# The first MoE's g from a ring of eight shared with the decoding's temporaries, its down products three feature tiles behind the up products

## The chip, the cores and the metric

One core of one Trainium2 chip runs the whole program. The metric is device time in microseconds (us) from one launch, of the slowest core, and here there is one. The engines are named as in the profile: PE (TensorE's matmuls), PEld (its weight loads), DVE (VectorE), ACT (ScalarE), POOL (GpSimd), SP (SyncE, which issues most DMAs). Each engine takes its instructions in the order in which they stand in its own queue; an instruction that waits holds up all behind it on that engine.

## What is computed

Three stages, each feeding the next. In the attention, a 40x40 state per head is decayed, corrected and updated at each of 768 steps, for 4 batches of 8 heads. Then a first MoE layer with one expert, and a second with four:

```python
for t in range(S):                                  # S = 768, D = 40
    y[:, :, t] = einsum('bhd,bhde->bhe', r_t, state)
    Sa = einsum('bhde,bhe->bhd', state, a_t)
    state = state * w_t[:, :, None, :] - outer(Sa, b_t) + outer(v_t, k_t)
x = y.transpose(0, 2, 1, 3).reshape(3072, 320)
h = x @ w_in                                        # 320 x 2048
g = h - tanh(h)
x = g @ w_out                                       # 2048 x 320
for e in range(4):                                  # second MoE, 320 x 1024 x 320 each
    out += p[:, e:e+1] * (maximum(x @ w1[e], 0) @ w2[e])
```

`w_in` and `w_out` arrive as 64-bit floats, and the kernel decodes them itself.

## The kernel before

The 768 steps of the attention are worked in chunks of 64, for two batches at a time: 24 chunks in all. Of each chunk there are a preparation (scans on DVE over w, line 200, after a clamp in line 263; the matrix products M of line 235), an inverse of a triangular matrix by columns on POOL (lines 299 and 301), the chain that carries the state (Z line 340, U 349, R 360, U again, T 390, S 371, in this order and from chunk to chunk), and the output (SC and Y, lines 418 to 435).

The first MoE works in blocks of 256 tokens, 12 blocks. A block has 16 feature tiles f of 128 features. `up(f)` puts eight matmuls (line 528) into a PSUM tile h, of which there are two (`psH`, line 80); ACT takes tanh of it into t (line 577); DVE forms t = h - t (line 578), which is the last reader of h; ACT copies t into gh, rounded (line 579); DVE forms the remainder gl = t - gh (line 580). `down(f)` multiplies gh and gl with the weights, six matmuls (line 591), into two accumulators of the block. gh and gl have three buffers each.

The products of the second MoE (lines 528 and 1011) follow when the first is done; that stage alone is about 700 us long.

The weights of the first MoE come in 32 pieces, an up and a down for each f. A piece is loaded (line 492), decoded by one ACT and four DVE instructions (lines 454 to 459) through temporaries t0 (two buffers), t1 and f2 (one each), rounded into a high part on ACT (line 471), and what is left is summed on PE by three products into a PSUM tile (`rest`, line 478), from which ACT copies the low part (line 479). The load of a piece waits for a mark that is written behind the high part of the piece three before it (lines 174 and 501).

The source emits these steps in slots: one chunk's chain, the preparation and inverse of later chunks, the output of an earlier one, and a share of the decoding (slots up to 1.75) or of the first MoE (from slot 2 on, lines 904 to 914), spread over the slot. The order in each engine's queue is not this order: the program is built with a scheduler (line 1093) that simulates the engines and takes, of what is ready there, what was emitted first. So a change of buffers or of the emitted order moves instructions of all stages against each other.

`moe1_all` (line 613) emits up(i) and then down(i - 2); `temps` (line 876) allots the decoding's temporaries. Both draw on the pool `mp`.

Of the kernel before, what the change touches and what calls it, by code (L numbers as in the profile page):

```python
# [12 lines left out]
F32R = mybir.dt.float32r  # L13
I32 = mybir.dt.int32
# [27 lines left out]
def tile_wkv_then_moe_then_moe(ctx, tc, r, k, v, w, a, b, moe_w_in, moe_w_out, probs, w1, w2, wT, aT, rT, kbT, vP, vT, wi_in, wo_in, out):  # L42
# [419 lines left out]
    def split_weights(raw, done, key, tag, temps):  # L462
        n = raw.shape[1] // words
        if f64:
            parts = decode(raw.rearrange("p (n two) -> p n two", two=2), *temps(n))
        else:
            parts = [temps(n)[0].bitcast(F32)]
            nc.vector.tensor_copy(out=parts[0], in_=raw)
        t = done[key] = wp.tile([128, 2, n], F32R, tag=tag, name=tag)
        hi, lo = t[:, 0], t[:, 1]  # L470
        nc.scalar.activation(out=hi, in_=parts[0], func=AF.Copy)
        return parts, hi, lo
# [47 lines left out]
    def fc1(ps, w_hi, w_lo, fs, x_hi, x_lo, ts_):  # L520
        lhs = lambda t, kk: t[:, kk, fs]
        rhs = lambda t, kk: t[:, kk, ts_]
        ops = []
        for kk in range(2):
            ops += [(lhs(w_hi, kk), rhs(x_hi, kk)), (lhs(w_hi, kk), rhs(x_lo, kk)), (lhs(w_lo, kk), rhs(x_hi, kk))]
        ops += [(lhs(w_hi, 2), rhs(x_hi, 2)), (lhs(w_lo, 2), rhs(x_hi, 2))]
        for i, (l, rr) in enumerate(ops):
            nc.tensor.matmul(ps, l, rr, start=(i == 0), stop=(i == len(ops) - 1))  # L528
# [15 lines left out]
    def moe1(mp, hf, bl):  # L544
        NTB = G * 128
# [24 lines left out]
        def up(f):  # L570
            ps = psH.tile([128, NTB], F32, tag="h", name="h")
            wi_hi, wi_lo = (wi_t[f][:, h].rearrange("p (k n) -> p k n", k=3) for h in range(2))
            fc1(ps, wi_hi, wi_lo, slice(0, 128), M["xh"], M["xl"], slice(0, NTB))
            t = mp.tile([128, NTB], F32, tag="t", name="t", bufs=2)
            gh = mp.tile([128, NTB], F32R, tag="gh", name="gh", bufs=3)
            gl = mp.tile([128, NTB], F32R, tag="gl", name="gl", bufs=3)
            nc.scalar.activation(out=t, in_=ps, func=AF.Tanh)  # L577
            nc.vector.tensor_tensor(out=t, in0=ps, in1=t, op=ALU.subtract)  # L578
            nc.scalar.activation(out=gh, in_=t, func=AF.Copy)  # L579
            nc.vector.tensor_tensor(out=gl, in0=t, in1=gh, op=ALU.subtract)  # L580
            M["g", f] = gh, gl
# [16 lines left out]
        def fin_b(tt):  # L598
# [10 lines left out]
            nc.sync.dma_start(out=x1T_d[256:DM, t0:t0 + 128], in_=x1T[0:KR, 2])  # L609

        return load, up, down, fin_a, fin_b, split

    def moe1_all(mp, blocks, weights):
        def add(fn, what):
            steps.append((lambda: (weights(what), fn())) if what else fn)

        fns = [moe1(mp, hf, bl) for hf, bl in blocks]
        steps = [fns[0][0], fns[0][5]]
        loads = [0]
        seq = [(n, f) for n in range(len(blocks)) for f in range(NF)]  # L620

        def down(n, f):
            add(lambda: fns[n][2](f), ("down", f) if n == 0 else None)
            if f == NF - 1:
                for tt in range(G):
                    steps.append(lambda tt=tt: fns[n][3](tt))
            if f == 1 and n > 0:
                for tt in range(G):
                    steps.append(lambda tt=tt: fns[n - 1][4](tt))

        for i, (n, f) in enumerate(seq):
            add(lambda n=n, f=f: fns[n][1](f), ("up", f) if n == 0 else None)
            if f == LOAD_F and n + 1 < len(blocks):
                loads.append(len(steps))
                steps.append(fns[n + 1][0])
            if f == NF - 1 and n + 1 < len(blocks):
                steps.append(fns[n + 1][5])
            if i >= 2:
                down(*seq[i - 2])
        down(*seq[-2])  # L640
        down(*seq[-1])
        for tt in range(G):
            steps.append(lambda tt=tt: fns[-1][4](tt))
        return steps, loads
# [226 lines left out]
    mp = one.enter_context(tc.tile_pool(name="mp", bufs=2, side="right"))  # L871
# [2 lines left out]
    nc.scalar.activation(out=minus, in_=ident, func=AF.Copy, scale=-1.0)  # L874

    def temps(n):
        kinds = (("t0", I32, 2), ("t1", I32, 1), ("f2", F32R, 1))
        return [mp.tile([128, 384], d, tag=t, name=t, bufs=k_)[:, 0:n] for t, d, k_ in kinds]

    dec, need = weights_steps(plus, minus, temps)  # L880
    done = [0]
# [6 lines left out]
    def share(i):  # L888
        k0, k1 = (max(0, int(len(dec) * (j - DEC_FROM) / (DEC_TO - DEC_FROM))) for j in (i, i + 1))
        return [lambda k=k: decoded(k + 1) for k in range(k0, min(k1, len(dec)))], 0, 1  # L890

    msteps, mloads = moe1_all(mp, blocks, lambda what: decoded(need[what]))

    def late_loads():
# [203 lines left out]
```

## Time and profile before

| what | value |
|---|---|
| median of 3 runs | 1610.53 us (1608.2 to 1612.03) |
| the profiled execution | 1613.03 us, of which the span, first to last instruction, is 1611.3 us |
| granted TensorE clock, mean | 0.948 of full speed |
| PE / DVE / POOL / ACT busy | 92 / 50 / 36 / 31 % of the span |
| first up product of the first MoE | at 194.0 us |
| last up product of the first MoE | at 903.6 us |

The profile comes from one execution. Its times count from the first instruction. A wait is idle time of an engine before an instruction, put down to the one that released it. The shares of busy time are averages over stages with different limits, so the stages are read one by one: to about 200 us (attention and decoding), 200 to 907 us (attention and first MoE; at the end the first MoE alone), and from 907 us the second MoE.

### The profile page before, as it was taken

The numbers are of one execution on the slowest core, as the hardware profiler recorded it, in microseconds if no ns is written. First come the engines' busy times: TensorE is split into PE (matmuls) and PEld (weight loads), VectorE is DVE, ScalarE is ACT, GpSimd is POOL, SyncE is SP. The second block draws the span as 40 slices with busy tenths as digits, with TensorE's granted clock in tenths as the row PEclk, the third lists the DMA queues.
The fourth block names the chain that finished last, engine by engine and source line by source line (L and its number), as shares of the span: only waits on it lengthen the run. The fifth ranks groups of instructions, "written<-read, shape, count | busy, mean of one in ns | idle before, by whom it ended". The sixth has DMA issues, their size and how long they took to land.

```text
span 1611.3 us, 33016 instructions
## 1 busy us (share of the span) xinstructions
PE 1478.0 (92%) x13178; PEld 1330.4 (83%) x13178; DVE 807.2 (50%) x1604; ACT 503.1 (31%) x1239; POOL 586.7 (36%) x1543
## 2 busy tenths in 40 slices
PE   3587898898989899989998999999999999999998
PEld 2366698888878788879998989898898989898997
DVE  8588756665656566666556443332333333332332
ACT  3344433333333333333345462121221212121111
POOL 4888865648485484665703001000000101010000
PEclk9578799999998999999999999999999999999999
DMA  4556522332432323232215331000010101000011
GB/s 127 130 151 158 132 50 72 97 83 69 101 86 77 82 69 95 76 94 66 61 39 156 101 100 29 8 21 17 1 36 1 37 1 36 1 1 1 0 50 51
DMA packets 163938, 103.26 MB, mean 64 GB/s; under 512 B 101952, under 2 KB 139840, under 8 KB 163776
## 3 DMA queue, kind: packets, MB, share of 16 engines
q1 hardware_dynamic: 97412, 71.64, 16.1%
q10 hardware_dynamic: 66364, 29.44, 7.6%
q8 instruction: 105, 1.72, 0.4%
q14 instruction: 57, 0.47, 0.1%
HBM read 82.82 MB, written 18.22 MB: 63 GB/s over the span
## 4 chain that ended last, share of the span: by engine, by line
PE 57%; DMA 6%; POOL 5%; DVE 3%; issue 3%; ACT 1%; SPq 0%; ACTq 0%; DVEq 0%; POOLq 0%
PE h L528 26%; PE acc L1011 21%; PE acc L591 4%; POOL Y L301 2%; POOL tmp L299 2%; PE SC L418 1%; DMA E<-in_wT_dram 1%; DMA N<-mt_d 1%; DMA TT<-tt_d 1%; PE SC L429 1%; DMA tt_d<-Y 1%; PE SC L433 1%; PE M L235 1%; DMA KBT<-in_kbT_dram 1%; PE Z L340 1%
## 5 line engine op out<-in xcount | busy, mean ns | idle before, releaser
L299 POOL TENSOR_TENSOR tmp<-Y,N 128x60 f32<-128x60 f32 (+24 forms) x744 | 254.8, 343 | 208.3 <-DMA N<-mt_d 108.9
L998 DVE SCALAR_TENSOR_TENSOR hl<-h,hh 128x512 fp32r<-128x512 f32 x192 | 132.1, 689 | 332.9 <-ACT hh L997 332.8
L301 POOL TENSOR_TENSOR Y<-Y,tmp 128x60 f32<-128x60 f32 (+24 forms) x744 | 264.7, 356 | 58.3
L997 ACT ACTIVATE hh<-h 128x512 fp32r<-128x512 f32 x192 | 114.6, 598 | 505.2 <-PE h L528 505.1
L528 PE MATMUL h<-xh,up 128*128 128x256 f32 x1152 | 236.9, 301 | 24.3 <-DVE t L578 14.2
L1011 PE MATMUL acc<-w2h,hh 128*128 128x320 f32 x768 | 236.3, 308 | 0.6 <-DVE oacc L1016 0.6
L1011 PE MATMUL acc<-w2l,hh 128*128 128x320 f32 x768 | 236.4, 308 | 0.0
L1011 PE MATMUL acc<-w2h,hl 128*128 128x320 f32 x768 | 235.3, 308 | 0.2 <-DVE hl L998 0.2
L528 PE MATMUL h<-xh,w1h 128*128 128x512 f32 x576 | 227.8, 395 | 0.0
L528 PE MATMUL h<-xh,w1l 128*128 128x512 f32 x576 | 227.1, 394 | 0.0
L947 POOL TENSOR_TENSOR w1l<-w1r,w1h 128x1536 fp32r<-128x1536 f32 x8 | 28.0, 3498 | 528.4 <-ACT w1h L946 528.4
L528 PEld LDWEIGHTS h<-xh,up 128*128 128x128 f32 x1152 | 188.6, 201 | 31.4 <-DVE t L578 17.7
L591 PE MATMUL acc<-down,gh 128*128 128x320 f32 x768 | 171.3, 321 | 3.1 <-ACT gh L579 3.1
L1011 PEld LDWEIGHTS acc<-w2l,hh 128*128 128x128 f32 x768 | 144.0, 188 | 12.0
L1011 PEld LDWEIGHTS acc<-w2h,hh 128*128 128x128 f32 x768 | 144.1, 188 | 11.6 <-DVE oacc L1016 1.0
L528 PE MATMUL h<-xl,w1h 128*128 128x512 f32 x384 | 151.7, 395 | 0.0
L1011 PEld LDWEIGHTS acc<-w2h,hl 128*128 128x128 f32 x768 | 143.7, 187 | 0.7 <-DVE hl L998 0.5
L1018 DVE SCALAR_TENSOR_TENSOR oacc<-acc,pnorm,oacc 128x320 f32<-128x320 f32 x168 | 84.4, 544 | 116.2 <-PE acc L1011 116.2
L591 PEld LDWEIGHTS acc<-down,gh 128*128 128x128 f32 x768 | 124.3, 194 | 6.3 <-ACT gh L579 4.1
L577 ACT ACTIVATE t<-h 128x256 f32<-128x256 f32 x192 | 72.4, 384 | 180.9 <-PE h L528 110.6
L580 DVE TENSOR_TENSOR gl<-t,gh 128x256 fp32r<-128x256 f32 x192 | 93.4, 491 | 69.0 <-ACT gh L579 67.7
L591 PE MATMUL acc<-down,gl 128*128 128x320 f32 x384 | 113.5, 324 | 14.0 <-DVE gl L580 14.0
(138 smaller groups left out, 2317.6 us busy)
## 6 DMA issues: line engine op xcount, KB each, us to landing
N<-mt_d SPq DMA_DIRECT2D x48, 256.0 KB
KBT<-in_kbT_dram ACTq DMA_DIRECT2D x46, 160.0 KB
raw_up<-in_wi_dram SPq DMA_DIRECT2D x16, 384.0 KB
raw_down<-in_wo_dram SPq DMA_DIRECT2D x16, 320.0 KB
w2r<-in_moe_w_dram SPq DMA_DIRECT2D x8, 640.0 KB
w1r<-in_moe_w_dram SPq DMA_DIRECT2D x16, 256.0 KB
xT_d<-yT SPq DMA_DIRECT2D x48, 80.0 KB
wchk<-in_w_dram SPq DMA_DIRECT2D x5, 768.0 KB
```

Of the source, the lines that this page charges most:

```text
L235: nc.tensor.matmul(ps[:, 128 * j:128 * j + 128], KBT[:, p], zs[:, :, p], start=True, stop=True)
L299: nc.gpsimd.tensor_tensor(out=tmp, in0=Y[:, 0:n, j:j + 1].to_broadcast([128, n, wd]), in1=nj.to_broadcast([128, n, wd]), op=ALU.mult)
L301: nc.gpsimd.tensor_tensor(out=Y[:, 0:n, j + 1:32], in0=Y[:, 0:n, j + 1:32], in1=tmp, op=ALU.subtract)
L528: nc.tensor.matmul(ps, l, rr, start=(i == 0), stop=(i == len(ops) - 1))
L577: nc.scalar.activation(out=t, in_=ps, func=AF.Tanh)
L580: nc.vector.tensor_tensor(out=gl, in0=t, in1=gh, op=ALU.subtract)
L591: nc.tensor.matmul(M["acc"][tt], l[:, cs], rr, start=(f == 0 and i == 0), stop=(f == NF - 1 and i == 2))
L947: nc.gpsimd.tensor_tensor(out=w1l, in0=w1r, in1=w1h, op=ALU.subtract)
L997: nc.scalar.activation(out=hh_, in_=ps, func=AF.Relu)
L998: nc.vector.scalar_tensor_tensor(out=hl_, in0=ps, scalar=0.0, in1=hh_, op0=ALU.max, op1=ALU.subtract)
L1011: nc.tensor.matmul(po, l[:, cs], rr[:, f], start=(f == 0 and i == 0), stop=(f == FH - 1 and i == 2))
L1018: nc.vector.scalar_tensor_tensor(out=oacc[:, n], in0=po, scalar=pe, in1=oacc[:, n], op0=ALU.mult, op1=ALU.add)
```

## The change

```diff
@@ -572,8 +572,8 @@
             wi_hi, wi_lo = (wi_t[f][:, h].rearrange("p (k n) -> p k n", k=3) for h in range(2))
             fc1(ps, wi_hi, wi_lo, slice(0, 128), M["xh"], M["xl"], slice(0, NTB))
             t = mp.tile([128, NTB], F32, tag="t", name="t", bufs=2)
-            gh = mp.tile([128, NTB], F32R, tag="gh", name="gh", bufs=3)
-            gl = mp.tile([128, NTB], F32R, tag="gl", name="gl", bufs=3)
+            gh = mp.tile([128, 384], F32R, tag="g", name="gh", bufs=8)[:, 0:NTB]
+            gl = mp.tile([128, 384], F32R, tag="g", name="gl", bufs=8)[:, 0:NTB]
             nc.scalar.activation(out=t, in_=ps, func=AF.Tanh)
             nc.vector.tensor_tensor(out=t, in0=ps, in1=t, op=ALU.subtract)
             nc.scalar.activation(out=gh, in_=t, func=AF.Copy)
@@ -635,8 +635,9 @@
                 steps.append(fns[n + 1][0])
             if f == NF - 1 and n + 1 < len(blocks):
                 steps.append(fns[n + 1][5])
-            if i >= 2:
-                down(*seq[i - 2])
+            if i >= 3:
+                down(*seq[i - 3])
+        down(*seq[-3])
         down(*seq[-2])
         down(*seq[-1])
         for tt in range(G):
@@ -874,8 +875,8 @@
     nc.scalar.activation(out=minus, in_=ident, func=AF.Copy, scale=-1.0)
 
     def temps(n):
-        kinds = (("t0", I32, 2), ("t1", I32, 1), ("f2", F32R, 1))
-        return [mp.tile([128, 384], d, tag=t, name=t, bufs=k_)[:, 0:n] for t, d, k_ in kinds]
+        kinds = (("t0", I32), ("t1", I32), ("f2", F32R))
+        return [mp.tile([128, 384], d, tag="g", name=t, bufs=8)[:, 0:n] for t, d in kinds]
 
     dec, need = weights_steps(plus, minus, temps)
     done = [0]
```

The temporaries t0, t1, f2 and the tiles gh and gl now take turns in one ring `g` of eight tiles of 128x384. Before, there were four temporaries of 384 and six g tiles of 256 columns, which is the same amount of memory. A piece of the decoding takes three tiles of the ring, a feature tile of the first MoE two, so that four feature tiles' g can be held where three could. down(i - 3) is emitted after up(i) in place of down(i - 2). No product, no copy and no DMA is added or removed.

The scheduler makes another order of it. Two places, as the queues stand (names carry the number of their buffer).

On DVE, in the third block of the first MoE around feature tiles 8 and 9. Before, t_4869 and gl_4871 belong to tile 8 and t_4912 to tile 9; L263, L200 and L210 are the preparation of a later chunk:

```order
L364 TENSOR_TENSOR Z_4514<-R_4680,Z_4514 32x320 x2
L578 TENSOR_TENSOR t_4869<-h_4860,t_4869 128x256
L263 TENSOR_SCALAR E2_117<-E2_117 128x8x64
L200 SCALAR_TENSOR_TENSOR RW_102<-E2_117,delta_92 128x260 x2
L210 RECIPROCAL start_103<-RW_102 40x8 x2
L200 SCALAR_TENSOR_TENSOR E2_117<-E2_117,start_103 128x260 x2
L580 TENSOR_TENSOR gl_4871<-t_4869,gh_4870 128x256
L578 TENSOR_TENSOR t_4912<-h_4903,t_4912 128x256
```

After, t_4863 and gl_4865 belong to tile 8, t_4906 and gl_4908 to tile 9:

```order
L364 TENSOR_TENSOR Z_4524<-R_4674,Z_4524 32x320 x2
L263 TENSOR_SCALAR E2_117<-E2_117 128x8x64
L200 SCALAR_TENSOR_TENSOR RW_102<-E2_117,delta_92 128x260 x2
L210 RECIPROCAL start_103<-RW_102 40x8 x2
L353 TENSOR_SCALAR vu0_93<-U_4739 32x8x40
L578 TENSOR_TENSOR t_4863<-h_4854,t_4863 128x256
L200 SCALAR_TENSOR_TENSOR E2_117<-E2_117,start_103 128x260 x2
L578 TENSOR_TENSOR t_4906<-h_4897,t_4906 128x256
L228 TENSOR_TENSOR KBT0_100<-KBT0_100,RW_102 128x512 x2
L580 TENSOR_TENSOR gl_4865<-t_4863,gh_4864 128x256
L580 TENSOR_TENSOR gl_4908<-t_4906,gh_4907 128x256
```

t of tile 9 now stands ahead of gl of tile 8, and both gl behind the whole preparation; the end of U (L353) stands ahead of both t.

On PE, in the chain of the first chunk, with the decoding's rest products (up_ is the high part of an up piece, down_ that of a down piece, t_ and f_ temporaries). Before, from R to S:

```order
L360 MATMUL R<-vu_93,MB_112 32x40 x16
L478 MATMUL rest<-up_647,minus 128x384
L478 MATMUL rest<-f_641,plus 128x384
L478 MATMUL rest<-t_675,ident 128x320
L349 MATMUL U<-Z,TT_125 32x40 x16
L478 MATMUL rest<-down_683,minus 128x320
L478 MATMUL rest<-f_677,plus 128x320
L478 MATMUL rest<-t_717,ident 128x384
L390 MATMUL T<-ident,vu_93 128x64 x8
L371 MATMUL S<-vu_93,KBn_108 40x40 x8
```

After, from the last rest products ahead of U to S:

```order
L478 MATMUL rest<-t_743,ident 128x320
L478 MATMUL rest<-down_751,minus 128x320
L478 MATMUL rest<-f_745,plus 128x320
L478 MATMUL rest<-t_788,ident 128x384
L349 MATMUL U<-Z,TT_125 32x40 x16
L478 MATMUL rest<-up_796,minus 128x384
L478 MATMUL rest<-f_790,plus 128x384
L478 MATMUL rest<-t_835,ident 128x320
L478 MATMUL rest<-down_843,minus 128x320
L478 MATMUL rest<-f_837,plus 128x320
L390 MATMUL T<-ident,vu_93 128x64 x8
L371 MATMUL S<-vu_93,KBn_108 40x40 x16
```

Of the 96 rest products, 31 stood ahead of T of the first chunk, and now 42; ahead of T of the second, third and fourth chunk it is 50, 61 and 79, and now 55, 73 and 87. The first up product stands behind 94 of them in both. But it stood behind R of the fifth chunk, and now within Z of that chunk, two chain steps earlier; and 14 feature tiles' up products now stand ahead of T of the fifth chunk, where it was 3. From the sixth chunk on the two orders are near each other again. In the last block, with no attention beside it, down(f) stands behind up(f + 2) in both.

## Rows read from the trace of the kernel before

**Rows 1.** The page: the span, and busy time of each engine.
```profile
span 1611.3 us, 33016 instructions
...
PE 1478.0 (92%) x13178; PEld 1330.4 (83%) x13178; DVE 807.2 (50%) x1604; ACT 503.1 (31%) x1239; POOL 586.7 (36%) x1543
```

**Rows 2.** Busy time by stretch: stretch, its us, engines, TensorE clock, DMA share, GB/s.
```profile
0.00:200.00 200.00, 134.51 (x1448) 101.78 (x1448) 149.36 (x305) 82.20 (x228) 152.76 (x390) 0.77 0.53 139
200.00:907.00 707.00, 646.89 (x7883) 601.92 (x7883) 428.52 (x900) 264.55 (x753) 395.09 (x1141) 0.95 0.32 79
...
140.00:160.00 20.00, 12.98 (x142) 11.33 (x142) 15.80 (x34) 6.25 (x18) 16.71 (x43) 0.80 0.58 149
160.00:180.00 20.00, 17.40 (x169) 12.43 (x165) 15.09 (x32) 8.96 (x25) 16.47 (x46) 0.52 0.47 130
180.00:200.00 20.00, 16.68 (x246) 13.26 (x244) 13.89 (x31) 9.06 (x22) 16.62 (x44) 1.00 0.53 130
```

**Rows 3.** TensorE waits, 200 to 800 us: us in total, times, longest.
```profile
PE h L528 <- DVE t L578: 13.8, 10, 5.4
PE acc L591 <- DVE gl L580: 10.2, 11, 2.9
...
PE acc L591 <- ACT gh L579: 2.8, 3, 1.8
```

**Rows 4.** VectorE in order of time, 349 to 355.5 us: start, us, instruction.
```profile
349.72 0.42 DVE L578 TENSOR_TENSOR t<-h,t 128x256 f32<-128x256 f32 x1
350.68 0.43 DVE L263 TENSOR_SCALAR E<-E 128x512 f32<-128x512 f32 x1 [0.53 <-DMA E<-in_wT_dram]
...
354.12 0.40 DVE L580 TENSOR_TENSOR gl<-t,gh 128x256 fp32r<-128x256 f32 x1
354.43 0.41 DVE L578 TENSOR_TENSOR t<-h,t 128x256 f32<-128x256 f32 x1
```

**Rows 5.** TensorE in order of time, three places: idle time in brackets.
```profile
354.57 0.56 PE L591 MATMUL acc<-down,gl 128*128 128x320 f32 x2 [2.23 <-DVE gl L580]
...
510.79 1.44 PE L591 MATMUL acc<-down,gh 128*128 128x320 f32 x4 [1.83 <-ACT gh L579]
...
655.12 0.90 PE L591 MATMUL acc<-down,gl 128*128 128x320 f32 x2 [2.94 <-DVE gl L580]
```

**Rows 6.** Granted TensorE clock (third from the end) in two stretches, as rows 2.
```profile
510.50:517.30 6.80, 6.30 (x23) 5.51 (x24) 4.18 (x11) 2.38 (x8) 0.00 (x0) 0.50 0.48 131
653.90:660.60 6.70, 5.48 (x24) 5.40 (x25) 4.00 (x10) 2.83 (x8) 5.37 (x18) 0.50 0.25 59
```

**Rows 7.** ScalarE and TensorE in order of time, 560 to 566 us.
```profile
562.95 0.66 ACT L577 ACTIVATE t<-h 128x256 f32<-128x256 f32 x2 [8.98 <-DMA N<-mt_d]
...
563.85 0.58 PE L528 MATMUL h<-xh,up 128*128 128x256 f32 x1 [5.36 <-DVE t L578]
```

**Rows 8.** TensorE waits, 800 to 910 us.
```profile
PE acc L591 <- DVE gl L580: 3.8, 2, 2.7
```

**Rows 9.** VectorE and GpSimd in order of time, 858 to 879 us.
```profile
862.28 3.47 DVE L580 TENSOR_TENSOR gl<-t,gh 128x256 fp32r<-128x256 f32 x1 [1.14 <-ACT gh L579]
...
862.02 3.45 POOL L947 TENSOR_TENSOR w1l<-w1r,w1h 128x1536 fp32r<-128x1536 f32 x1 [59.46 <-ACT w1h L946]
```

**Rows 10.** TensorE waits for the decoding, 0 to 200 us.
```profile
PE rest L478 <- ACT down L471: 10.2, 4, 5.4
PE rest L478 <- DVE t L456: 8.2, 8, 2.3
...
PE rest L478 <- ACT up L471: 3.3, 3, 2.7
...
PE h L528 <- ACT down L479: 2.5, 1, 2.5
```

**Rows 11.** Lines 454 and 528: ns min/median/max, first to last start, in us.
```profile
L454 ACT ACTIVATE t<-raw_up x16: 524/552/568, 11.4 to 183.0; 128x384 f32<-128x384 f32 x16
...
L528 PE MATMUL h<-xh,up x1152: 274/283/583, 194.0 to 903.6; 128*128 128x256 f32 x192
```

## Prediction

> **What bounds the kernel now.** I read the page first for the whole, then the busy time by stretch, then TensorE's waits by stretch, and last the engines in order of time around single waits. PE is busy for 92% of the span, DVE for half of it [rows 1]. In the order of the stages: to 200 us PE stands idle for 200 - 134.5 = 65.5 us, and POOL works 16.5 to 16.7 of each 20 us, so it is POOL's inverses that set how fast chunks come there [rows 2]. From 200 to 907 us PE is idle for 707 - 646.9 = 60.1 us at a mean granted clock of 0.95 [rows 2]: this stretch is bound by PE's own work and by the short waits inside it, and a us of idle time that goes there comes off the end, since the second MoE only follows. The change touches the second MoE nowhere, so what is decided is decided before 907 us.
>
> The waits that the change speaks of are those of the down products: 10.2 us for gl and 2.8 us for gh between 200 and 800 us, 13.0 us in 14 waits [rows 3]. Beside them the up products wait 13.8 us in 10 waits for t, that is, for one of the two h tiles to be read [rows 3].
>
> **Term 1, the waits of the down products.** The three largest are of three kinds. At 354.6 us PE waits 2.23 us for gl [rows 5]: DVE did t at 349.7, then took up a preparation that waited for a DMA and ran to 354.1, then gl, and the next t only behind it [rows 4]. At 655.1 us it waits 2.94 us, at the end of a block, and at 510.8 us 1.83 us for gh, an ACT matter [rows 5]. Would one more tile of distance cover such a wait? With the old order on DVE, hardly: up(f + 3) needs the h tile that t of f + 1 frees, and that t stood behind the late gl (gl done 354.1 + 0.4 = 354.5, t done 354.8 [rows 4]), so PE would have got 0.9 us of other work and then stood before an up product in place of a down product. But the new order on DVE is another: in the first place shown of the change, t of two tiles in a row stand ahead of both gl, so the h tiles come free without gl, and the down products that wait for gl stand behind more up products. That covers the first kind. The second kind has the end of a block and a late load in it, the third a late ACT; I count these as not surely covered. So I take half of the 13.0 us: 6.5 us, with 0 and 13.0 as the ends.
>
> To this comes the clock. In the 6.8 us around the waits at 510.8 and 655.1 us the granted clock is 0.50, the lower of TensorE's two levels, 1.2 GHz in place of 2.4 [rows 6]; each such stretch gives back half its length, 3.4 us, if PE doesn't stop ahead of it. I take one of the two, 3.4 us, with 0 and 6.8 us as ends. Term 1 is 9.9 us of gain, between 0 and 19.8.
>
> From 800 to 910 us 3.8 us of waits for gl stay [rows 8]: there the order of up and down products is the same before and after. What made them is in the trace: a gl of 128x256 takes 3.47 us from 862.28 on, where others take 0.40 [rows 4, 9], while POOL runs one subtraction of 3.45 us from 862.02 on [rows 9]. The Trainium skill, page "SBUF — State Buffer", section "SBUF: two separate sides", says of this that VectorE instructions with two SBUF inputs and GpSimd instructions that read SBUF lock the same pair of ports for their whole length; by that rule a ring of g cannot shorten it, and the trace agrees. It leaves the sum as it is.
>
> **Term 2, waits of the up products.** What is not waited for at a down product can come back at an up product: both hang on the same DVE and ACT queues. The largest such wait, 5.36 us at 563.8 us, comes from ACT standing for 8.98 us before tanh [rows 7]; there two full h tiles stop PE whatever g's ring holds, but for one more down product that is left to do. The trace has no row for the new order, so the ends are a loss of the 6.5 us that term 1 took back, and a gain of half of the 13.8 us, 6.9 us, if the t that now stand earlier on DVE free h sooner. I take a loss of 2 us, nearer to nothing than to the lower end: of the ten waits for t [rows 3] the long one shown is ACT's doing, which the order on DVE doesn't touch.
>
> **Term 3, the decoding.** Its pieces go through three of eight ring tiles in place of fixed temporaries, so f2 of a piece no longer waits for PE's sum of the piece before it. The same number of instructions runs. The scheduler answers by putting the decoding earlier against the attention: 42 in place of 31 rest products ahead of the first chunk's T. Now the decoding ends and the first up product starts at 194.0 us [rows 11]; the 16 up pieces start between 11.4 and 183.0 us [rows 11], 171.6 / 30 = 5.7 us for a piece. If it ends earlier, the first MoE fills PE's idle time: from 140 to 200 us that is 7.0 + 2.6 + 3.3 = 12.9 us [rows 2], and that is the upper end. If it doesn't, PE, which takes its queue in order, stands before rest products that are not ready: it did so for 10.2 + 8.2 + 3.3 + 2.5 = 24.2 us already [rows 10], and half as much again, 12.1 us, is my lower end. POOL sets the pace of the chunks here and its order does not depend on the ring, so neither end is near; I take 0.
>
> **The sum.** 9.9 - 2.0 + 0 = 7.9 us of gain. The profiled execution took 1613.0 us (span 1611.3 and 1.7 us around it), so it would take 1605.1 us; the median of the runs is 2.5 us lower, 1610.5, and 7.9 us off it give 1602.6 us.
>
> **The rivals.** *It is h, not g, that is short.* The two h tiles bound how far PE runs ahead, g's ring does not, and each us saved at a down product is lost at the next up product. For it speaks that waits for t are as large as those for gl and gh together, 13.8 against 13.0 us [rows 3], and the place at 354 us with DVE's old order; against it speaks DVE's new order. The Trainium skill, page "Perfetto Trace Analysis", section "Optimization Strategy", says that gaps which come again and again on the engine that should be full can mean too little SBUF or PSUM for the next tile; by it the gap belongs to whichever ring is short, and the trace has both kinds. Time: no change, 1610.5 us. Chance 0.20.
>
> *Slower: the decoding stands in the chain's way.* In PE's queue the first chunk's T now stands behind 11 more rest products, that is 11 / 3 = 3.7 pieces, and 3.7 x 5.7 = 21 us at the old pace. If the pace stays, the chains of the first four chunks wait on PE for it, chunk five's T comes behind 14 feature tiles, and the lost time on PE is the 12.1 us of above, 1622.6 us. For it speaks that PE already waits 24.2 us for decoding [rows 10]; against it that the chain has room behind POOL, and that PE finds the first MoE's work ahead of T of chunk five. It decides from the start of the first up product: later than 194 us with PE's waits for rest grown, this rival holds. Chance 0.23.
>
> *Faster by much: the decoding ends earlier as well.* Term 1 as taken and term 3 at its upper end: 9.9 - 2.0 + 12.9 = 20.8 us, 1589.7 us. For it speaks that f2's wait is gone and that each engine's queue has the decoding earlier; against it that the loads still wait for the piece three before. Chance 0.13.
>
> **How the numbers follow.** The forecast has 0.44, around 1602.6 us, from 1597 to 1607 with its own bounds. Faster by over 0.2% (3.2 us, about what a measurement of this kernel tells from no change) come the forecast and the last rival, 0.57; within it the first rival, 0.20; slower the second, 0.23. The range leaves out 0.2 of the chances: from 1589, where the last rival lies, to 1619, short of the full price of the slower one.
>
> **What would show it.** Right: waits for gl and gh between 200 and 800 us at some 6 us in place of 13.0, those for t at 13 to 17, fewer stretches at clock 0.50, the first up product within 5 us of 194. The first rival: gl and gh down, t up by as much, PE idle from 200 to 907 us still near 60. The slower one: waits for rest of 30 us and more, the first up product after 200 us, the first MoE's last product after 907. The last: the first up product ahead of 185 us. The forecast is wrong as a whole if PE's idle time after 200 us moves by waits that no term names, for the new order moves all stages: waits of the chain for DVE and for loads.

## The result and the profile after

The changed kernel takes 1621.22 us (median of 5 runs, 1618.53 to 1621.56), the kernel before 1610.53; the ratio is 1.0062, 95% interval 1.0045 to 1.008. So it is slower by 0.6%, where 1602.6 us was forecast, and 2 us outside the range. The profiled execution has a span of 1619.8 us against 1611.3 [rows 1].

TensorE's waits of the changed kernel between 200 and 800 us (us in total, times, longest), to be read against [rows 3]:

```profile
PE h L528 <- DVE t L578: 28.0, 13, 5.9
PE T L390 <- DVE vu L353: 20.0, 6, 5.8
...
PE acc L591 <- DVE gl L580: 1.4, 2, 1.3
```

The wait for gl, 10.2 us in [rows 3], is 1.4 us, and none for gh is left. But the up products wait 28.0 us for t in place of 13.8. And the chain's T (line 390) waits 20.0 us for vu, of which the same view of before has this:

```profile
PE T L390 <- DVE vu L353: 8.0, 6, 4.2
```

Busy time by stretch and TensorE's clock (third from the end), as [rows 2], and the first and last up product, as [rows 11]:

```profile
0.00:200.00 200.00, 125.58 (x1290) 94.08 (x1290) 145.00 (x296) 78.18 (x223) 141.34 (x375) 0.78 0.51 132
200.00:907.00 707.00, 644.36 (x7982) 604.23 (x7982) 427.50 (x901) 263.53 (x749) 403.68 (x1157) 0.94 0.32 82
...
L528 PE MATMUL h<-xh,up x1152: 274/283/583, 196.9 to 912.4; 128*128 128x256 f32 x192
```

These waits do not add up to the loss. Others fell by 11.8 us: those of the up products for xh (4.8 and 2.3 us, now none), of SC for DVE (2.5, now none), of U for Z (6.7, now 5.4) and 0.9 us of Z without a releaser. So PE's idle time from 200 to 800 us went from 54.2 to 57.1 us only, and from 200 to 907 us from 60.1 to 62.6. To 200 us it is 200 - 125.6 = 74.4 us, where it was 65.5; but here executions of one order scatter. Runs below that keep an order up to about 200 us (of the experiments with `LAG` and `INV_CUT` for the old one, with four and three tiny loads for the new one) give 68.0 and 70.7 us for the old one, 69.7 and 73.4 for the new one. What holds in all six is U's wait for the load of TT, 18.3 to 19.9 us in the new order, 11.6 to 12.9 in the old.

The first up product comes 2.9 us later than in [rows 11] (in two other executions of the new order at 193.7 and 192.8 us, so this is scatter), the last 8.8 us later. In between the profiled execution was not behind: the eighth of the twelve blocks ends (its first copy of line 596) at 720.8 us, before at 724.0. The ninth ends at 788.3, before at 781.0. The third block, with a stand ahead of 350 us that is shown below, loses as much, 74.1 us long in place of 64.7; but the blocks up to the eighth win that back. The ninth is what stays lost, and the loss shows in one stretch of it, here before and then after:

```profile
720.00:740.00 20.00, 19.23 (x202) 18.03 (x202) 14.03 (x31) 9.47 (x28) 16.57 (x44) 1.00 0.16 39
740.00:760.00 20.00, 19.68 (x292) 18.15 (x290) 10.49 (x25) 7.49 (x21) 7.25 (x27) 1.00 0.39 100
```

```profile
720.00:740.00 20.00, 18.62 (x198) 17.63 (x197) 13.37 (x30) 9.77 (x29) 16.32 (x48) 0.91 0.20 45
740.00:760.00 20.00, 14.09 (x195) 12.89 (x192) 6.27 (x14) 3.60 (x10) 7.00 (x24) 0.85 0.27 61
```

From 740 to 760 us PE is idle for 5.9 us, before for 0.3, and its clock is 0.85, before 1.00. The engines in order of time (start, us, instruction, idle time before it in brackets; ACTq and SPq are the queues' own steps, DMA issues here):

```profile
742.28 0.84 ACTq L248 DMA_DIRECT2D mt_d<-MB  x2
743.16 0.43 ACT L352 ACTIVATE vu<-U 32x320 f32<-32x320 f32 x1 [0.51 <-PE U L349]
743.24 8.17 ACTq L248 DMA_DIRECT2D mt_d<-MB  x2
...
748.83 0.37 SPq L306 DMA_DIRECT2D tt_d<-Y  x1
751.13 0.58 SPq L310 DMA_DIRECT2D TT<-tt_d  x1
...
751.51 4.20 ACTq L152 DMA_DIRECT2D rd<-in_rT_dram  x2
755.80 0.38 ACT L577 ACTIVATE t<-h 128x256 f32<-128x256 f32 x1 [12.21 <-DMA TT<-tt_d]
...
756.70 0.58 PE L528 MATMUL h<-xh,up 128*128 128x256 f32 x1 [5.91 <-DVE t L578]
```

ACT has 12.21 us without work. It is not out of work: tanh stands in its queue behind four stores of MB and two loads of rd, and two of these six issues do not go out. The fourth store has gone out by 743.24 + 8.17 = 751.4, 2.6 us after SP's store of the inverse (748.83), the second load of rd by 755.7, 4.6 us after SP's load of TT (751.13). Nothing in the data ties them to these transfers. I call this "ACT stands". The changed kernel has five such stands of 9.3 to 12.2 us between 200 and 910 us; the kernel before has three of over 7 us, 8.98 us at most [rows 7].

The stand ahead of 350 us shows how T's waits grow from it:

```profile
342.02 0.37 SPq L306 DMA_DIRECT2D tt_d<-Y  x1
344.32 0.58 SPq L310 DMA_DIRECT2D TT<-tt_d  x1
...
344.69 4.51 ACTq L248 DMA_DIRECT2D mt_d<-MB  x2
349.30 0.72 ACTq L152 DMA_DIRECT2D E<-in_wT_dram  x2
...
348.22 0.76 PE L349 MATMUL U<-Z,TT 32*32 32x40 f32 x32
...
351.97 0.43 DVE L263 TENSOR_SCALAR E<-E 128x512 f32<-128x512 f32 x1 [5.70 <-DMA E<-in_wT_dram]
...
354.20 0.50 DVE L353 TENSOR_SCALAR vu<-U 32x320 f32<-32x320 f32 x1
...
354.75 0.69 PE L390 MATMUL T<-ident,vu 64*128 64x64 f32 x8 [5.77 <-DVE vu L353]
```

PE had U ready by 349. The load of E stood on ACT behind a store of MB until 349.3, so DVE waited 5.70 us for E in the preparation of a later chunk. The copy of U (line 353) stood behind that on DVE, and T behind the copy on PE.

What stayed: from 800 to 910 us the down products wait 3.6 us for gl, as in [rows 8].

```profile
PE acc L591 <- DVE gl L580: 3.6, 3, 2.4
```

### The profile page after: what moved, and what is told of

Same layout as the page of the kernel before. It is cut to its first block, busy times and chain, and to the rows that moved or that the text cites. A ratio compares the mean times of both kernels' runs of the same rounds, so it can differ in the third digit from the quotient of the medians.

```text
span 1619.8 us, 32999 instructions
## 1 busy us (share of the span) xinstructions
PE 1474.5 (91%) x13178; PEld 1333.2 (82%) x13178; DVE 805.4 (50%) x1604; ACT 502.0 (31%) x1239; POOL 583.8 (36%) x1543
## 4 chain that ended last, share of the span: by engine, by line
PE 51%; DMA 1%; DVE 0%; ACT 0%; issue 0%; SPq 0%; ACTq 0%; DVEq 0%
PE h L528 25%; PE acc L1012 21%; PE acc L591 3%; PE SC L418 0%; DMA w2r<-in_moe_w_dram 0%; PE SC L433 0%; PE SC L429 0%; PE U L349 0%; DMA TT<-tt_d 0%; DMA xr<-x1T_d 0%; PE Z L340 0%; PE S L371 0%; DVE gl L580 0%; PE x1T L602 0%; DMA tt_d<-Y 0%
## 5 line engine op out<-in xcount | busy, mean ns | idle before, releaser
L528 PE MATMUL h<-xh,up 128*128 128x256 f32 x1152 | 240.8, 306 | 29.6 <-DVE t L578 29.0
L528 PEld LDWEIGHTS h<-xh,up 128*128 128x128 f32 x1152 | 192.2, 206 | 36.1 <-DVE t L578 32.1
L948 POOL TENSOR_TENSOR w1l<-w1r,w1h 128x1536 fp32r<-128x1536 f32 x8 | 28.1, 3514 | 529.0 <-ACT w1h L947 529.0
L591 PE MATMUL acc<-down,gh 128*128 128x320 f32 x768 | 176.7, 322 | 0.3 <-ACT gh L579 0.3
L1012 PEld LDWEIGHTS acc<-w2l,hh 128*128 128x128 f32 x768 | 144.0, 188 | 12.1
L1012 PEld LDWEIGHTS acc<-w2h,hh 128*128 128x128 f32 x768 | 144.1, 188 | 10.7
L591 PEld LDWEIGHTS acc<-down,gh 128*128 128x128 f32 x768 | 127.6, 195 | 2.6 <-ACT gh L579 0.5
L578 DVE TENSOR_TENSOR t<-h,t 128x256 f32<-128x256 f32 x192 | 79.7, 422 | 100.0 <-ACT t L577 97.9
L528 PEld LDWEIGHTS h<-xh,w1l 128*128 128x128 f32 x576 | 108.3, 188 | 21.8
```

Source lines behind the costliest of these rows:

```text
L591: nc.tensor.matmul(M["acc"][tt], l[:, cs], rr, start=(f == 0 and i == 0), stop=(f == NF - 1 and i == 2))
L948: nc.gpsimd.tensor_tensor(out=w1l, in0=w1r, in1=w1h, op=ALU.subtract)
L1012: nc.tensor.matmul(po, l[:, cs], rr[:, f], start=(f == 0 and i == 0), stop=(f == FH - 1 and i == 2))
```

## The experiments

Four theories stood against each other. **Decoding** (D): the earlier decoding is in the chain's way, the prediction's slower rival. **Order** (N): the order before is a lucky one, and any other costs as much. **SP** (Q): SP is short, since a store that waits for POOL holds up its other transfers. **Shared semaphores** (S): ACT stands because of a semaphore. The last rests on a list of the built program. Each DMA counts up a semaphore when it lands; those of SP and ACT take eight of them in turn, in the order of the program. So each has the semaphore of the DMA eight places ahead of it, on whichever engine, and its issue waits until that one has landed. The place near 743 us, place in the sequence first:

```
604 SP  L306 tt_d<-Y          semaphore 104
605 ACT L152 VUT<-in_vT_dram  semaphore 105
606 ACT L152 VUT<-in_vT_dram  semaphore 107
607 SP  L310 TT<-tt_d         semaphore 108
608 SP  L291 Y<-eye_d         semaphore 109
609 ACT L248 mt_d<-MB         semaphore 101
610 ACT L248 mt_d<-MB         semaphore 102
611 ACT L248 mt_d<-MB         semaphore 103
612 ACT L248 mt_d<-MB         semaphore 104
613 ACT L152 rd<-in_rT_dram   semaphore 105
614 SP  L441 xT_d<-yT         semaphore 107
615 ACT L152 rd<-in_rT_dram   semaphore 108
```

The two issues that stood are those that share with the inverse's store (104) and with the load of TT (108). In the built program each of the two waits for that one semaphore and for nothing else. Of 907 such DMAs, 32 of ACT's share so with an L306 or L310 of SP in the changed kernel, 31 in the kernel before: it is not their number that grew.

**Each part alone.** First the lag alone: g in two rings of four of its own, and the temporary t1 put where the pool had room (excerpt, against the kernel before).

```diff
-            gh = mp.tile([128, NTB], F32R, tag="gh", name="gh", bufs=3)
+            gh = mp.tile([128, NTB], F32R, tag="gh", name="gh", bufs=4)
(gl likewise)
-            if i >= 2:
-                down(*seq[i - 2])
+            if i >= 3:
+                down(*seq[i - 3])
+        down(*seq[-3])
-        kinds = (("t0", I32, 2), ("t1", I32, 1), ("f2", F32R, 1))
+        kinds = (("t0", "t0", I32, 2), ("t1", "spare", I32, 3), ("f2", "f2", F32R, 1))
```

> The lag alone: gh and gl each four deep in rings of their own, down(i - 3); the decoding keeps its temporaries (its t1, which only DVE uses, moves to the spare ring to make room). In PE's queue the decoding stands as in the kernel before (31 rest products ahead of the first T). Theory L (the loss of 10.7 us comes after 200 us, from what the lag does to the order of ACT, DVE and PE): 1616 to 1623 us, waits for gl and gh from 200 to 800 us under 4 us, waits of up for t and of T for vu over 35 us together (before: 13.8 + 8.0). Theory D (the decoding ahead in the queue costs it, the rival of the prediction): 1607 to 1613 us, as before or a little faster.

Measured: 1622.64 us, ratio 1.0059 (1.004 to 1.0078), with the first up product at 194.4 us. TensorE's waits between 200 and 800 us:

```profile
PE h L528 <- DVE t L578: 23.2, 8, 5.5
PE T L390 <- DVE vu L353: 16.2, 4, 8.1
...
PE acc L591 <- DVE gl L580: 4.5, 3, 3.1
```

Then the ring alone: the changed kernel with `down(*seq[i - 2])` as before.

> The ring alone: t0, t1, f2, gh and gl in the ring of eight as in the changed kernel, but down(i - 2). In PE's queue the decoding stands as in the changed kernel (42 rest products ahead of the first T, 14 feature tiles ahead of the fifth). Theory L: 1607 to 1614 us, near the kernel before; PE's work by 210 us is what it was. Theory D: 1616 to 1623 us, with waits for rest of 28 us in the first 200 us and a loss that is there by 300 us.

Measured: 1620.48 us, 1.0047 (1.0026 to 1.0068). The waits, same view:

```profile
PE h L528 <- DVE t L578: 22.1, 8, 7.1
...
PE Z L340 <- ACT gh L579: 9.1, 1, 9.1
PE acc L591 <- DVE gl L580: 8.1, 8, 2.5
```

Either part alone costs as much as both. (L, in these two expectations, says that the loss comes from the lag, after 200 us.) The two runs do not part the theories. For the lag alone theory L's time came, with waits for gl just above what I had set; but the waits for rest in the first 200 us grew there too, from 10.2 + 8.2 + 3.3 = 21.7 us [rows 10] to 37.8, though 31 rest products stand ahead of the first T as before. For the ring alone all that theory D forecast came: the time, waits for rest of 11.8 + 9.7 + 3.8 + 2.8 = 28.1 us, and a first block that ends at 262.8 us, before at 255.8. What speaks against D comes below: kernels with the decoding as early as here, and 30 to 46 us faster. Both runs have stands of over 11 us (12.42 and 12.41; 11.03), which lead here to T's wait for vu, there to Z's wait behind gh.

**The order.** The kernel before with one number of its plan changed: `LAG = 1.3` for 1.25, then `INV_CUT = 8` for 7.

> The kernel before with the first MoE's steps emitted 0.05 slot later against the attention (LAG 1.3 in place of 1.25): no buffer and no distance is changed, and the scheduler makes another order from about the second block on. Theory N (any other order is some 0.5% slower than the one that the kernel before happens to have, whatever the reason): 1616 to 1624 us. Theory S: stands of ACT over 7 us may come or go; 1606 to 1624 us, slower where their sum over 200 to 800 us is larger.

> The kernel before with 8 in place of 7 columns of each inverse emitted one slot earlier: the order on POOL stays, that on the other engines moves a little. Theory N: 1616 to 1624 us. Otherwise within 4 us of the kernel before.

Measured: 1612.89 us, 1.0004 (0.9994 to 1.0015), and 1614.84 us, 1.0013 (0.9999 to 1.0028). Theory N wanted 1616 us or more and falls; the second is a weak test, as SP, POOL and DVE have the same order in it as before. The first also shows that a stand has no fixed price: it has three, of 9.74, 12.20 and 9.59 us, and loses nothing, where I had expected a longer time with a larger sum of stands. Its waits:

```profile
PE h L528 <- DVE t L578: 24.8, 11, 5.7
...
PE T L390 <- DVE vu L353: 2.2, 2, 1.6
```

Then `LAG = 1.3` in the changed kernel:

> The changed kernel with the planner's LAG 1.3 instead of 1.25: another order of the decoding with no other purpose. Theory S says that the changed kernel's loss depends on which DMA of ACT falls behind which DMA of SP, so that another order draws other stands: it may come out anywhere from 1605 to 1630 us, and the sum of T's waits for vu and the up products' waits for t (48.0 us) moves by as much as the time. Theory D (the decoding that comes earlier is in the chain's way, whatever its detail) gives 1617 to 1625 us, as the changed kernel.

Measured: 1610.69 us, 0.9989 (0.9972 to 1.0005); its waits for t are 8.2 us, T's for vu 12.6. So another order of the same change is 10.5 us better, and the 0.6% is not the price of ring and lag in every order. The sum of the two waits fell by 27.2 us, not by as much as the time, as I had expected.

**Store and load of the inverse issued by POOL**, in four kernels: the changed one, the one before, lag alone, ring alone.

```diff
-            nc.sync.dma_start(out=bass.AP(dst.tensor, dst.offset, [[32, 128], [4096, 8], [1, 32]]), in_=Y)
+            nc.gpsimd.dma_start(out=bass.AP(dst.tensor, dst.offset, [[32, 128], [4096, 8], [1, 32]]), in_=Y)
-            nc.sync.dma_start(out=TT.rearrange("p h t -> p (h t)"),
+            nc.gpsimd.dma_start(out=TT.rearrange("p h t -> p (h t)"),
```

> The changed kernel, with the store of the inverse (tt_d) and the load of TT issued by POOL in place of SP, so that no DMA that ACT issues shares its landing semaphore with a transfer that waits for POOL's inverse. Theory S (ACT's DMA issues stand for up to 8 us until such a transfer of SP lands, and tanh behind them; the new order pays more for that): faster than the changed kernel by 8 us or more, 1600 to 1613 us, and no ACT idle time over 9 us between 300 and 800 us (five before: 9.3 to 12.2). If these stands are not what costs, 1618 to 1630 us, as POOL has two more issues and a wait for the store in each of 24 chunks.

> The same in the kernel before. Theory S, where the stands cost both kernels alike: 1598 to 1606 us. Where the stands cost only the changed kernel: 1609 to 1615 us.

> The lag alone (gh and gl four deep in own rings, down(i - 3), the decoding's temporaries as before), with tt_d's store and TT's load on POOL. Theory S (ACT's stands hide a gain of the lag): the gain that showed when the changed kernel lost its stands is the lag's: 1580 to 1592 us, and waits for gl and gh from 200 to 800 us under 5 us (18.8 us in the kernel before with the same move). If the gain belongs to the ring and the earlier decoding: 1600 to 1608 us.

> The ring alone (down(i - 2)), with tt_d's store and TT's load on POOL. Theory S with the gain in the lag: 1600 to 1608 us. If the gain belongs to the ring and the earlier decoding: 1580 to 1592 us. If it needs both: both of these two near 1600.

| | SP | POOL |
|---|---|---|
| before | 1610.53 | 1606.19 (0.9941) |
| lag alone | 1622.64 (1.0059) | 1594.49 (0.9886) |
| ring alone | 1620.48 (1.0047) | 1606.41 (0.9944) |
| both: the change | 1621.22 (1.0062) | 1580.62 (0.979) |

(In brackets the ratio to the kernel before; the intervals reach 0.002 to 0.004 to either side. The kernel before, measured beside each run, took 1610.5 to 1614.5 us, so times of different runs compare to some 4 us, and the ratios are better.) The changed kernel came out 19 us below the range of theory S, the lag alone 2.5 us above its own. In the right column the lag gains 11.7 us, the ring alone nothing, and both 25.6 us; by the ratios 0.6%, 0 and 1.5%. Theory D falls here as the one cause: 43 rest products stand ahead of the first T of this changed kernel, 42 did without the edit. The waits of the changed kernel with this edit, and its up products:

```profile
PE h L528 <- DVE t L578: 22.5, 12, 3.5
PE T L390 <- DVE vu L353: 8.6, 3, 3.2
...
L528 PE MATMUL h<-xh,up x1152: 274/283/584, 175.2 to 873.3; 128*128 128x256 f32 x192
```

and those of the kernel before with it, which still waits for gl:

```profile
PE acc L591 <- DVE gl L580: 18.8, 11, 3.3
PE h L528 <- DVE t L578: 13.3, 4, 6.3
```

**Which of the transfers.** The changed kernel with only the stores of MB (line 248) from ACT to POOL, SP as it was; then with only the store of Y (line 306) from SP to POOL; then with both.

> The changed kernel, with the decoding's stores of MB to mt_d (L248) issued by POOL instead of ACT; SP keeps the inverse's store and the load of TT. Theory S (ACT stands at an issue whose landing semaphore an unfinished DMA of SP still holds, and the tanh and U's copy stand behind it): the five stands of 9.3 to 12.2 us that the changed kernel has lose their first part, the waits of T for vu (20.0 us) and of the up products for t (28.0 us) fall by 8 us or more together, time 1590 to 1613 us. Theory Q (SP itself is what is short: a store that waits for POOL holds up SP's other transfers): nothing is changed on SP, time 1617 to 1625 us. Third way: POOL, which now issues the stores, stands itself and the inverse is late: slower than 1625 us.

> The changed kernel, with the store of Y to tt_d (L306) alone issued by POOL; SP keeps the load of TT, which waits for that store as before. Theory S: the stands that end at a DMA behind the store go (near 743 and 613 us of the changed kernel), those behind the load of TT (near 345, 414, 549, 751 us) stay, so part of the 40 us between the changed kernel and the one with both on POOL (1580.6): 1595 to 1615 us. Theory Q: SP still waits at the load of TT until the inverse's result has been stored, so as long as before: 1617 to 1625 us.

> The changed kernel with both the store of Y to tt_d and the decoding's stores of MB to mt_d on POOL. Theory S (ACT stands at shared semaphores): each of the two moves alone gave 1575.4 and 1591.0 us; what stands are left with the first are at most 5.6 us, so little is left to gain: 1568 to 1585 us. If the moves help in another way, by taking issues off ACT and SP, they add up: below 1560 us. If POOL's own issues come late: above 1590 us.

Measured: 1591.01 us, 0.9866 (0.9828 to 0.9903); 1575.38 us, 0.9776 (0.9753 to 0.9798), the best of all; 1583.38 us, 0.979 (0.9755 to 0.9825). The first leaves SP's transfers on SP and gains 30 us, so theory Q falls as the one cause. The second gained more than I expected (1595 to 1615 us), and the third not the sum, so the gain does not come from taking issues off ACT and SP. The second, by stretch, first the changed kernel as it is, then with the edit:

```profile
200.00:800.00 600.00, 542.87 (x6939) 508.21 (x6939) 368.78 (x785) 216.38 (x625) 382.61 (x1123) 0.93 0.32 81
```

```profile
200.00:800.00 600.00, 565.04 (x7475) 530.60 (x7474) 385.69 (x822) 227.96 (x664) 404.37 (x1160) 0.97 0.32 83
...
L528 PE MATMUL h<-xh,up x1152: 274/283/584, 174.7 to 860.1; 128*128 128x256 f32 x192
```

PE's idle time falls from 57.1 to 35.0 us, and the clock rises from 0.93 to 0.97. No stand is over 5.7 us. The last up product comes 52.3 us earlier than in the changed kernel, but the first comes 22.2 us earlier already, ahead of the five stands (with store and load of TT on POOL it is 39.1 and 21.7 us). What brings it forward was not tested by itself. The kernel before with the same edit:

> The kernel before with the inverse's store of Y to tt_d (L306) alone issued by POOL: the pair to the changed kernel with that edit (1575.4 us), so that what ring and lag are worth is read where ACT stands least. If they are worth some 1.6% there, as with store and load of TT on POOL: 1595 to 1610 us. If the move alone makes the gain and ring and lag nothing: 1572 to 1585 us.

Measured: 1606.79 us, 0.9947 (0.992 to 0.9975). So ring and lag are worth 1606.8 - 1575.4 = 31.4 us there, by the ratios 1.7%.

**Other semaphores for the same transfers.** All moves to POOL also change the scheduler's order. The last runs leave each transfer on its engine and add tiny loads on SP that nobody reads, which turn on the semaphores of what follows. First eight behind each load of TT, in the changed kernel and in the one before; these change the order of all engines too, from the first chunks on (code shortened):

```diff
+    turn = [const.tile([1, 8], F32, name=f"turn{i}") for i in range(8)]
...
             nc.sync.dma_start(out=TT.rearrange("p h t -> p (h t)"),
                               in_=bass.AP(src.tensor, src.offset, [[256, 4], [1024, 32], [1, 256]]))
+            for i in range(8):
+                nc.sync.dma_start(out=turn[i], in_=bass.AP(src.tensor, src.offset, [[8, 1], [1, 8]]))
```

> The changed kernel with eight tiny loads of no use behind each load of TT (192 DMAs more, all on SP). The DMAs of ACT that share their semaphore with the inverse's store or load of TT just before them go from 32 to 4. Theory S: no stand of ACT of over 8 us is left, T's waits for vu fall from 20.0 to below 10 us, time 1585 to 1610 us although SP has 192 issues more (some 0.4 us each). Theory Q: SP has more to do, 1621 to 1640 us.

> The kernel before with the same eight tiny loads behind each load of TT; the DMAs of ACT that share a semaphore with store or load of TT go from 31 to 10. Theory S: what the kernel before gained when store and load went to POOL (1606.2 us), so 1600 to 1610 us, and less than the gain of the changed kernel, since the down products still wait for gl with three buffers of it. Theory Q: 1612 to 1630 us.

Measured: 1585.64 us, 0.982 (0.979 to 0.985), and 1602.18 us, 0.9925 (0.9903 to 0.9948). 192 useless transfers make the changed kernel 2.2% faster than it was. As expected, no stand over 8 us is left after 200 us (the longest idle time of ACT, 8.77 us, ends at PE's U and not at a DMA); but T waited 13.6 us for vu, where I had expected less than 10. The kernel before has one stand of 10.41 us with this edit. Here ring and lag are worth 16.5 us, 1.1% by the ratios.

Then four of them behind the 14th load of TT alone, where the order of every engine is word for word that of the changed kernel; and three ahead of the 22nd, where it is the same up to that place.

> The changed kernel with four of the tiny loads behind the 14th load of TT alone. The order of every engine is word for word that of the changed kernel, and as many DMAs of ACT share a semaphore with store or load of TT as there (32). Both theories: 1617 to 1625 us, as the changed kernel; a time below 1615 us would mean that tiny loads on SP help for another reason than the semaphores, and the two runs with them would show nothing.

> The changed kernel with three tiny loads (32 bytes each, of no use) that SP issues just before the 22nd load of TT, near 750 us. The order of all engines is the same up to there; the semaphores that the later DMAs take turn on by three, so that of the stores of MB and loads of rd near 743 to 755 us none shares one with the inverse's store or load of TT. Theory S (the shared semaphore makes ACT stand): ACT's stand of 12.21 us at 755.8 us falls below 5 us, the wait of 5.91 us for t at 756.7 us goes, and the time is 1612 to 1617 us, 4 to 9 less than the changed kernel. Theory Q (SP is what is short): three more transfers on SP, 1619 to 1624 us.

Measured: the four, 1618.64 us, 1.0038 (1.0019 to 1.0056): as the changed kernel, with the same five stands (9.2 to 12.7 us) and a ninth block that ends at 788.7 us. So four tiny loads do nothing by themselves. The three, 1612.51 us, 0.9992 (0.9967 to 1.0017): in the range of theory S, but not by what it said, for the stand is still there. (The issue at 748.20 is the second of the two in the first line, from a view that starts later.)

```profile
736.66 11.85 ACTq L248 DMA_DIRECT2D mt_d<-MB  x2
...
747.05 0.84 SPq L309 DMA_DIRECT2D turn<-tt_d  x3
...
748.20 0.31 ACTq L248 DMA_DIRECT2D mt_d<-MB  x1
...
749.67 0.66 ACT L577 ACTIVATE t<-h 128x256 f32<-128x256 f32 x2 [12.66 <-DMA rd<-in_rT_dram]
```

The list of this program says why. The fourth store of MB now has the semaphore (108) of the first tiny load, which waits for the inverse's store, and it went out at 748.2, 1.1 us behind the tiny load. That is the clearest sight of the mechanism: a store on ACT held for a 32-byte load on SP with which it has nothing in common but the semaphore. This kernel has all five stands (9.8 to 12.7 us) and is not slower than the kernel before; why is not settled. Its ninth block takes 64.3 us, in the changed kernel 67.4 and before 56.9, so the price of the last stand is there; but its profiled execution was 4.7 us ahead of the changed kernel's at the end of the eighth block (716.1 us), before its order differs.

**A third h.** The changed kernel with store and load on POOL, `psA` with `bufs=3` for 4 and `psH` with `bufs=3` for 2.

> The changed kernel with store and load of the inverse on POOL (1580.6 us), with three buffers for h instead of two and three for the decoding's products instead of four. In the kernel without this step the up products still wait 22.5 us for t in 200 to 800 us, twelve times, 3.5 us at most. If h is short there (the rival that h, not g, is what the first MoE lacks), these waits fall by 10 us or more and the time to 1568 to 1575 us, less what the decoding's products then wait for a bank. If the waits come from ACT and DVE being late altogether, a third h moves them to the next product: 1578 to 1590 us.

Measured: 1602.17 us, 0.993 (0.9906 to 0.9953), slower than both forecasts. The expectation has one thing wrong: the tiles of `psA` are not the decoding's but those of the attention's products (M, Z, U, R, S, T, SC); the decoding's rest products take turns in `psH` with h. So the edit gives h a tile and takes one from the attention, which makes the rows of x that xh is copied from. The waits for t fall from 22.5 to 7.4 us, and another takes their place, for xh, whose rows come late:

```profile
PE h L528 <- ACT xh L565: 40.8, 7, 8.8
```

Whether the third h or the attention's missing tile made xh late, this run does not show.

## Why the prediction was wrong

**Term 1, the waits of the down products, held.** 13.0 us were to become about 6; they became 1.4 us. In the kernels with shorter stands the lag alone is worth 11.7 us, ring and lag together 16.5 to 31.4 us. The term's share for the clock did not come: 0.94 after 200 us in place of 0.95, as new stretches of low clock came with the new waits (0.85 from 740 to 760 us, before 1.00).

**Term 2 is the step that failed.** The up products' waits for t were to cost 2 us, 6.5 at worst; they rose by 28.0 - 13.8 = 14.2 us. The argument was that DVE's order frees h sooner and that the one long wait was ACT's doing, "which the order on DVE doesn't touch". But the change moves ACT's order too, and with it what stands behind ACT's DMA issues. The stand of 8.98 us was in [rows 7], and I read it as one wait among ten, not as a kind that each new order deals out again. The wait for gh at 510.8 us [rows 5], which I took for a late ACT of another kind, also stood behind one:

```profile
509.39 0.38 ACT L577 ACTIVATE t<-h 128x256 f32<-128x256 f32 x1 [8.12 <-DMA tt_d<-Y]
```

Stands are not all of it. In the three pairs of kernels with the same edit for the semaphores, ring and lag raise the waits for t as well, from 13.3 to 22.5, 11.2 to 22.1 and 14.4 to 18.5 us. That part is what the first rival said, a wait that moves from the down to the up product, and term 2 had given it 2 us.

**A wait that no term named.** T's wait for vu rose by 12.0 us, through a late load of E and DVE's queue. [rows 4] had its small form, 0.53 us before the same preparation. The last sentence of the prediction allowed for this ("waits of the chain for DVE and for loads"), the sum did not. Together: 11.6 us of waits for g gone, 14.2 + 12.0 = 26.2 us come, and 11.8 us of others gone that no term named either, so PE's idle time after 200 us is not what these terms would make it.

**Term 3, taken as 0, was near only by its mark.** The first up product came at 196.9 us, within 5 of 194; the waits for rest were 13.0 + 9.2 + 3.0 + 2.7 = 27.9 us, below the 30 of the slower rival. But PE's idle time to 200 us grew by 8.9 us in the profiled executions, within the 12.1 us of the term's lower end, and U waited some 6 us longer for TT in all of them. And I took 0 because POOL sets the pace, which other kernels here do not bear out. With ring and POOL's issues the first up product comes at 175 to 178 us, past the 185 us that were the last rival's mark, and with the stores of MB and Y both on POOL at 152.1. It pays only with the lag: with the ring alone, 177.9 us for the first and 907.4 for the last, and no gain.

**The rivals.** *Slower* had the time right (1622.6 us). The sign that was to decide it came in the profiled execution (first up product after 194 us, waits for rest above 24.2 us), and the last product came after 907 us; the 30 us and the 200 us did not. As the one cause it falls, since the decoding is as early in kernels 30 to 46 us faster; that it has a part in the loss is not excluded. *It is h that is short* is half right: the waits for t did rise as g's fell, but with the stands shorter the change gains though the waits for t are still 22.1 us. *Faster by much* has the mechanism of the best kernels: earlier decoding plus the lag, 1580.6 and 1575.4 us.

The Trainium skill, page "DMA: Bandwidth & Descriptors", section "Issuing engines are not separate DMA queues", says that starting DMAs on several engines saves only the sequencer's time to start them, usually little. By this a move of two issues to POOL should have given next to nothing; it gave 40.6 us. The runs do not speak against the rule about the DMA engines themselves, since eight tiny loads on SP gave 35.6 us without any move: what both edits change, beside the order, is which transfer an issue waits for, of which the section says nothing.

What stays open: how much each stand cost, and so how much of the 10.7 us is the stands'. That a shared semaphore makes ACT stand is shown; the price is argued from one stretch of two executions and from edits that gain 30 to 46 us, more than the 10.5 us that another order alone gave. Another order of the same change takes 1610.7 us with stands of up to 9.2 us, the kernel before with three of 9.6 to 12.2 us no more than without them, and all edits but the four tiny loads changed the order beside the semaphores.

## What to carry to other kernels

Before pricing a change that reorders, list the long idle times that end at a DMA, on engines that issue DMAs themselves, and ask what each issue waits for. If it is a semaphore shared with another engine's late transfer, move or pad that transfer first. Only then did the deeper buffer show its worth here: time up by 0.6% without the edit, down by 1.1 to 1.7% with it, against the kernel before with the same edit. And treat such a stand as something that every new order deals again: what it costs depends on what stands behind it in the queue. Before calling a sum of waits the cause, check it against the engine's whole idle time: here two waits grew by 26.2 us and the idle time after 200 us by 2.5.

## What was not expected

- A DMA issue on ACT waited over 7 us for a transfer of SP that has none of its data, because the two are eight places apart in the list of DMAs.
- 192 useless loads of 32 bytes made the kernel faster, 1621.2 to 1585.6 us.
- TensorE's clock over 200 to 800 us was 0.93 with 57.1 us of idle time and 0.97 with 35.0 us.
